# Nine score groups a batch with a shared third bank pair, and a reordered first batch, in a fused attention and feed-forward kernel

## The chip, the cores and the metric

One core of one Trainium2 chip. The metric is the device time of one execution in microseconds (us), as a median over several executions; most of them agree within 0.3%. A *call* is a session in which several kernels were timed in turn, in rounds, on one chip. Engines are named as in the profile: PE is TensorE's matmul stream and PEld its weight loads, ACT is ScalarE, DVE is VectorE, POOL is GpSimd, and SP is the queue that issues most transfers. Batches, head pairs and groups are counted from 0.

## The reference, cut to what matters

```python
# q, k, v: (8 batches, 12 heads, 448 positions, 64)
q_n = q / (norm(q) + 1e-6);  k_n = k / (norm(k) + 1e-6)
attn = softmax(q_n @ k_n.T / 0.1)
x = (attn @ v) -> (8 * 448 tokens, 768)
out = gelu(x @ w_in) @ w_out          # 768 -> 2048 -> 768
```

A batch has 12 heads, that is 6 head pairs. Each pair has 4 chunks of keys, so a batch has 24 scores. A score is two matmuls (one for each head of the pair) and one exp of 112x896.

## The kernel before: the parts that the change touches

Each of the batches 1 to 7 is an attention stage followed by the first layer of the feed-forward block (`hp`). The second layer (`op`) of earlier batches is cut into single matmuls, the *filler*, and is laid between the attention's pieces, so that TensorE has work while ScalarE computes exps. The scores go into bank pairs of TensorE's accumulator memory, two of them before the change:

```python
def scores(g, c0, n=2):                       # n scores of pair g
    qkT = qkT_t[g]
    for c in range(c0, c0 + n):
        st = ps_st.tile([128, 2, 512], F32, tag="st", ...)     # 2 buffers
        ... two matmuls into st ...
        pt = ptp.tile([CS, 2, S], BF16, tag="pt", ...)
        nc.scalar.activation(pt, st[:CS, :, :S], AF.Exp, scale=inv_tau)

def both(g, aside):                           # pairs g and g + 1
    columns(g, 0)                             # sums: 16 matmuls against ones
    reciprocals(g)                            # VectorE: transpose, reciprocal, transpose
    columns(g, 1)                             # first half of o = pt @ v
    columns(g, 2, aside=aside)                # second half
    normalise(g)                              # VectorE: x = o * reciprocal

def attention(b, fill):
    plan = {96: ((18, 8), (8, 8), (0, 10), (8, 8), (0, 10), (8, 10)),   # filler, odd batches
            128: ((22, 8), (13, 12), (0, 12), (12, 12), (0, 12), (12, 13))}[len(fill)]
    nxt = (b + 1) * HP
    for i in range(HP):                       # i: pair of the batch
        g = b * HP + i
        if i > 0:
            scores(g, 0)
        ...
        upto(scale, min(g + 4, nxt))          # GpSimd: q, k times 1/norm, up to three pairs on
        upto(transposes, min(g + 4, nxt))     # DMA transposes of them
        upto(square, nxt + min(max(i - late, 0), 3))
        run(plan[i][0])                       # filler
        if i in (2, 4):
            both(g - 2, ...)
        upto(reduce, nxt + min(max(i - 1 - late, 0), 3))
        scores(g, 2)
        if i in (0, 3):
            upto(load_v, g // 3 + 3, NV)      # values of three pairs, issued by GpSimd
        ... # loads of q and k
        run(plan[i][1])
    upto(reduce, nxt + 3); roots(2 * b + 7); both(nxt - 2, 1)

def first(b):                                 # first layer; at its end:
    ...
    scores(nxt, 0); roots(2 * b + 8)          # the next batch starts, then logarithm and root
```

`upto(f, n)` emits the next steps of `f` until n of them are out, so its place in the program fixes the place of the work in its engine's order. `square`, `reduce`, `roots` and `scale` prepare a pair; the prepared pair is then transposed by a DMA (`qkT<-qkb`). The 4 chunks of pair 3 are the batch's scores 12 to 15.

## Time and profile before

| what | before |
|---|---|
| median of 3 runs | 440.19 us (439.91 to 441.44) |
| first layer of batch 0 starts | 38.52 us |
| attention of batches 1, 3, 5, 7 (96 filler matmuls) | 30.5 to 30.6 us each |
| attention of batches 2, 4, 6 (128 filler matmuls) | 35.31 us each |
| mean granted clock of TensorE | 0.999 |

"Attention" is the time from the first score of a batch to its first matmul of the first layer.

### The profile page before, as it was taken

What the parts mean: (1) busy time and instruction counts of PE and PEld (TensorE: products, weight loads), DVE (VectorE), ACT (ScalarE), POOL (GpSimd) and SP (SyncE); (2) the same over time, 40 slices, a digit from 0 to 9 for tenths busy, and PEclk for the clock granted to TensorE, in tenths of its full rate; (3) what the DMA queues carried; (4) which work ended last, traced back from release to release, by engine and by line L of the source; (5) the groups of instructions that cost most, each with busy time, mean ns of one, the idle gap of its engine ahead of it and who ended that gap; (6) DMA issues with size and microseconds to landing.
All of it is one profiled execution on the core that took longest, in us unless ns stands there. A gap on an engine that the chain in (4) does not pass through costs nothing.

```text
span 438.1 us, 7927 instructions
## 1 busy us (share of the span) xinstructions
PE 426.8 (97%) x3294; PEld 215.7 (49%) x3294; DVE 164.8 (38%) x266; ACT 264.0 (60%) x380; POOL 203.3 (46%) x185
## 2 busy tenths in 40 slices
PE   7789999999999999999999999999999999999996
PEld 4344554445445554455544545445444554445563
DVE  4776313641355305552154501753055421341021
ACT  4796587646666467744767359655766457773300
POOL 2899834491834609291571906655190722300000
PEclk9999999999999999999999999999999999999999
DMA  9999999946683909766295843748077600911022
GB/s 201 237 241 209 180 178 211 265 105 135 109 160 88 226 4 114 171 119 149 29 159 134 159 109 53 172 121 208 1 130 153 134 2 1 132 43 31 1 72 72
DMA packets 83635, 54.97 MB, mean 125 GB/s; under 512 B 41872, under 2 KB 78608, under 8 KB 83600
## 3 DMA queue, kind: packets, MB, share of 16 engines
q1 hardware_dynamic: 66416, 42.35, 43.4%
q0 software_dynamic: 16784, 11.80, 19.1%
q8 instruction: 25, 0.41, 0.4%
q10 hardware_dynamic: 400, 0.33, 0.2%
q14 instruction: 10, 0.08, 0.1%
HBM read 45.61 MB, written 11.01 MB: 129 GB/s over the span
## 4 chain that ended last, share of the span: by engine, by line
PE 90%; DMA 5%; POOL 2%; DVE 1%; ACT 1%; SPq 0%; issue 0%; DVEq 0%
PE op L268 35%; PE hp L433 33%; PE st L206 11%; PE o L228 7%; PE sm L228 4%; DMA qk<-in_k_dram 3%; DMA v<-in_v_dram 2%; POOL qkb L176 1%; POOL sq L137 1%; SPq L107 0%; ACT pt L209 0%; DVE nq L149 0%; DVE x L246 0%; DVE rs L239 0%; DVE ot L279 0%
## 5 line engine op out<-in xcount | busy, mean ns | idle before, releaser
L209 ACT ACTIVATE pt<-st 112x896 bf16<-112x896 f32 x192 | 165.1, 913 | 50.0 <-PE st L206 49.6
L268 PE MATMUL op<-wo,g 128*128 128x384 bf16 x896 | 157.9, 327 | 0.0
L433 PE MATMUL hp<-x,wi 128*128 128x448 bf16 x768 | 147.0, 353 | 0.2 <-DVE x L246 0.2
L455 ACT ACTIVATE g<-hp 128x448 bf16<-128x448 f32 x128 | 66.9, 545 | 89.9 <-PE hp L433 89.6
L268 PEld LDWEIGHTS <-g 128*128 128x128 bf16 x896 | 81.9, 98 | 70.0 <-issue 21.0
L433 PEld LDWEIGHTS <-wi 128*128 128x128 bf16 x768 | 74.5, 98 | 72.1 <-issue 3.7
L176 POOL TENSOR_TENSOR qkb<-qk,rn 112x512 bf16<-112x512 f32 x95 | 96.8, 1045 | 11.8 <-DVE rn L167 11.7
L137 POOL TENSOR_TENSOR sq<-qk 112x1024 f32<-112x1024 f32 x44 | 82.3, 1888 | 5.8 <-DMA qk<-in_k_dram 5.6
L165 POOL TENSOR_SCALAR se<-sr 112x48 f32<-112x48 f32 x14 | 4.6, 326 | 150.2 <-ACT sr L164 150.2
L149 DVE TENSOR_REDUCE nq<-sq 112x16 f32<-112x1024 f32 x47 | 57.0, 1214 | 38.7 <-POOL sq L137 38.6
L206 PE MATMUL st<-qkT 64*112 64x448 bf16 x384 | 59.7, 374 | 2.6 <-ACT pt L209 1.9
L279 DVE COPY ot<-op 128x384 f32<-128x384 f32 x55 | 29.8, 543 | 79.2 <-PE op L268 79.2
L167 DVE RECIPROCAL rn<-se 112x48 f32<-112x48 f32 (+1 forms) x20 | 7.9, 393 | 99.7 <-POOL se L165 99.4
L228 PE MATMUL o<-pt,v 112*32 112x448 bf16 x768 | 41.8, 353 | 1.0 <-DMA v<-in_v_dram 1.0
L206 PEld LDWEIGHTS <-qkT 64*112 64x112 bf16 x384 | 21.5, 124 | 38.3 <-issue 34.5
L246 DVE TENSOR_TENSOR x<-o,rs 128x448 bf16<-128x448 f32 x48 | 27.8, 620 | 5.0 <-PE o L228 2.7
L228 PEld LDWEIGHTS <-v 112*32 112x32 bf16 x768 | 20.3, 97 | 17.1 <-DMA v<-in_v_dram 1.2
L235 DVE STREAM_TRANSPOSE tr<-sm 128x448 f32<-128x448 f32 x24 | 15.5, 646 | 34.8 <-PE sm L228 34.8
L228 PE MATMUL sm<-pt,ones 112*32 112x448 bf16 x384 | 23.1, 355 | 0.0
L323 PE MATMUL spin<-blank,ident 112*112 112x448 bf16 x46 | 13.3, 439 | 2.9 <-DVE qkT L194 1.5
L239 DVE STREAM_TRANSPOSE rs<-rc 128x448 f32<-128x448 f32 x24 | 15.5, 645 | 0.8
L120 POOL DMA_DIRECT2D v<-in_v_dram x17 | 14.0, 823 | 0.0
(37 smaller groups left out, 80.0 us busy)
## 6 DMA issues: line engine op xcount, KB each, us to landing
qk<-in_q_dram SPq DMA_DIRECT2D x48, 224.0 KB, 5.8
qk<-in_k_dram SPq DMA_DIRECT2D x47, 224.0 KB, 6.1
v<-in_v_dram POOLq DMA_DIRECT2D x15, 336.0 KB, 6.8
wi<-in_moe_w_in_dram POOLq DMA_DIRECT2D x4, 768.0 KB, 11.5
wo<-in_moe_w_out_dram POOLq DMA_DIRECT2D x4, 768.0 KB, 20.7
out_dram<-ot SPq DMA_DIRECT2D x7, 336.0 KB, 3.5
out_dram<-ot SPq DMA_DIRECT2D x8, 288.0 KB, 2.6
out_dram<-ot SPq DMA_DIRECT2D x8, 240.0 KB, 3.0
```

Source lines behind the costliest of these rows:

```text
L137: nc.gpsimd.tensor_tensor(sq, t, t, ALU.mult)
L149: nc.vector.tensor_reduce(nq, sq, mybir.AxisListType.X, ALU.add)
L176: eng.tensor_tensor(qkb[:, i].rearrange("p c h d -> p h c d"), t[:, i], rn[:, i].to_broadcast([CS, 2, NC, D]), ALU.mult)
L206: nc.tensor.matmul(st[:CS, h, :S], lhsT=qkT[rows, 1, c, :], rhs=qkT[rows, 0, :, :], start=True, stop=True)
L209: nc.scalar.activation(pt, st[:CS, :, :S], AF.Exp, scale=inv_tau)
L228: nc.tensor.matmul(bank_t[g, n][r:r + 32, :S], lhsT=w, rhs=pt_t[g + j, c][:, h, :], start=(c == 0), stop=(c == NC - 1), tile_position=(0, r))
L235: nc.vector.transpose(tr.rearrange("p b r -> p (b r)"), bank_t.pop((g, 0))[:, :S])
L246: nc.vector.tensor_tensor(x_t[b][:, p + n - 1, :], bank_t.pop((g, n))[:, :S], rs, ALU.mult)
L268: nc.tensor.matmul(ps[:, :NH], lhsT=g_t[sb][:, kf, t * 128:(t + 1) * 128], rhs=wo[:, kf, ni * NH:(ni + 1) * NH], start=(kf == 0), stop=(kf ...
L279: nc.vector.tensor_copy(ot[:, lo:hi], ps[:, :NH])
L433: nc.tensor.matmul(hps[m], lhsT=wi[:, kd, m * 128:(m + 1) * 128], rhs=x_t[b][:, kd, :], start=(kd == order[0]), stop=(kd == order[-1]))
L455: nc.scalar.activation(g_t[sb][:, m, hf * S:(hf + 1) * S], hps.pop(m), AF.Gelu)
```

## The change

The intent: fewer and larger groups of scores (3, 3, 2, 3, 2, 3, 3, 2, 3 instead of twelve of 2), so that fewer waits for exps stand in TensorE's stream. The third score of a group needs a third bank pair. It gets none of its own but shares the pair that the sums and the first half of o take, which become two halves of one tile. The filler plan is new. In the first batch, copies go ahead of roots, three spins (matmuls on zeros that only keep TensorE going) are dropped, and a value load moves into an idle time.

```diff
+    def scores(g, c0, count=2):
+        for n in range(count):
+            score(*divmod(g * NC + c0 + n, NC), n == 2)
+    def score(g, c, third):
+            pool = ps_acc if third else ps_st
+            st = pool.tile([128, 2, 512], F32, tag="third" if third else "st", ...)
 ...
     def columns(g, n, chunks=range(NC), aside=0):
+        if chunks[0] == 0 and n == 0:
+            so = ps_acc.tile([128, 2, 512], F32, tag="third", name=f"so{g}")
+            bank_t[g, 0], bank_t[g, 1] = so[:, 0], so[:, 1]
 ...
     def both(g, aside):
         columns(g, 0)
+        columns(g, 1)
         reciprocals(g)
-        columns(g, 1)
 ...
-        plan = {96: ((18, 8), (8, 8), (0, 10), (8, 8), (0, 10), (8, 10)), ...
+        plan = {96: (13, 7, 10, 7, 11, 11, 9, 10, 18),
+                128: (25, 14, 13, 14, 11, 12, 10, 10, 19)}[len(fill)]
 ...
+        for k, count in enumerate((3, 3, 2, 3, 2, 3, 3, 2, 3)):
+            if k > 0:
+                scores(b * HP, n, count)
+            if k in (4, 7):
+                both(b * HP + (0 if k == 4 else 2), ...)
+            upto(reduce, nxt + (due if late else (0, 0, 0, 0, 1, 1, 2, 3, 3)[k]))
+            for i in range(-(-n // NC), -(-(n + count) // NC)):   # pairs whose first score is in the group
+                ... scale, transposes, square, load_v, load_qk as before ...
+            n += count
+            run(plan[k])
 ...
-            scores(nxt, 0)
+            scores(nxt, 0, 3)
             roots(2 * b + 8)
 ... # first batch:
-                upto(reduce, 4)
                 roots(3)
                 upto(scale, 3)
+                upto(load_wi, 1)
 ...
-            upto(load_v, (2, 3, 3, 3, 3, 4)[g], NV)
+            upto(load_v, (3, 3, 3, 3, 3, 4)[g], NV)
 ...
+    upto(load_v, 2, NV)
+    upto(transposes, 1)
+    spin(2)
     roots(2)
     upto(scale, 2)
-    upto(load_v, 2, NV)
-    upto(load_wi, 1)
-    upto(transposes, 1)
-    spin(5)
+    upto(load_v, 3, NV)
```

More of the change, by code (lines that the diff above doesn't have):

```diff
@@ L197, in transposes @@
             nc.vector.tensor_copy(qkT, tp)
-    def scores(g, c0, n=2):
-        qkT = qkT_t[g]
-        for c in range(c0, c0 + n):
-            st = ps_st.tile([128, 2, 512], F32, tag="st", name=f"st{g}_{c}")
+    def scores(g, c0, count=2):
+        for n in range(count):
+            score(*divmod(g * NC + c0 + n, NC), n == 2)
+    def score(g, c, third):
+            qkT = qkT_t[g]
+            pool = ps_acc if third else ps_st
+            st = pool.tile([128, 2, 512], F32, tag="third" if third else "st", name=f"st{g}_{c}")
             for h in range(2):
@@ L219, in columns @@
     def columns(g, n, chunks=range(NC), aside=0):
-        if chunks[0] == 0:
-            bank_t[g, n] = (mm_tile(f"o{g + 1}", aside=aside) if n == 2 else
-                            ps_acc.tile([128, 512], F32, tag=("sm", "o")[n], name=("sm", "o")[n] + str(g)))
+        if chunks[0] == 0 and n == 0:
+            so = ps_acc.tile([128, 2, 512], F32, tag="third", name=f"so{g}")
+            bank_t[g, 0], bank_t[g, 1] = so[:, 0], so[:, 1]
+        elif chunks[0] == 0 and n == 2:
+            bank_t[g, 2] = mm_tile(f"o{g + 1}", aside=aside)
         for c in chunks:
@@ L380, in attention @@
         fill = list(fill)
-        plan = {96: ((18, 8), (8, 8), (0, 10), (8, 8), (0, 10), (8, 10)),
-                128: ((22, 8), (13, 12), (0, 12), (12, 12), (0, 12), (12, 13))}[len(fill)]
+        plan = {96: (13, 7, 10, 7, 11, 11, 9, 10, 18),
+                128: (25, 14, 13, 14, 11, 12, 10, 10, 19)}[len(fill)]
         def run(n):
@@ L389, in attention @@
         nxt = (b + 1) * HP
-        for i in range(HP):
-            g = b * HP + i
-            if i > 0:
-                scores(g, 0)
-            late = 2 if b == 1 else 0
-            if i == HP - 1 and not late:
-                roots(2 * b + 7)
-            upto(scale, min(g + 4, nxt))
-            upto(transposes, min(g + 4, nxt))
-            upto(square, nxt + min(max(i - late, 0), 3))
-            run(plan[i][0])
-            if i in (2, 4):
-                both(g - 2, 0 if len(fill) % KF else 1)
-            upto(reduce, nxt + min(max(i - 1 - late, 0), 3))
-            scores(g, 2)
-            if i in (0, 3):
-                upto(load_v, g // 3 + 3, NV)
-            if late and i == 2:
-                upto(load_qk, nxt + 4)
-            if i in (3, 4):
-                upto(load_qk, nxt + i + 2)
-            run(plan[i][1])
+        late = 2 if b == 1 else 0
+        n = red = due = 0
+        for k, count in enumerate((3, 3, 2, 3, 2, 3, 3, 2, 3)):
+            if k > 0:
+                scores(b * HP, n, count)
+            if k in (4, 7):
+                both(b * HP + (0 if k == 4 else 2), 0 if len(fill) % KF else 1)
+            upto(reduce, nxt + (due if late else (0, 0, 0, 0, 1, 1, 2, 3, 3)[k]))
+            due = red
+            for i in range(-(-n // NC), -(-(n + count) // NC)):
+                g = b * HP + i
+                if i == HP - 1 and not late:
+                    roots(2 * b + 7)
+                upto(scale, min(g + 4, nxt))
+                upto(transposes, min(g + 4, nxt))
+                upto(square, nxt + min(max(i - late, 0), 3))
+                if i in (0, 3):
+                    upto(load_v, g // 3 + 3, NV)
+                if late and i == 2:
+                    upto(load_qk, nxt + 4)
+                if i in (3, 4):
+                    upto(load_qk, nxt + i + 2)
+                red = min(max(i - late, 0), 3)
+            n += count
+            run(plan[k])
         upto(reduce, nxt + 3)
```

## The prediction

> **What bounds the kernel now.** I read the page first, then the chain that ended last, then TensorE's timeline stage by stage, then the timeline of all engines around one narrow wait. The page says who is full, from start to end and at full clock:
>
> ```profile
> PE 426.8 (97%) x3294; PEld 215.7 (49%) x3294; DVE 164.8 (38%) x266; ACT 264.0 (60%) x380; POOL 203.3 (46%) x185
> PE   7789999999999999999999999999999999999996
> PEclk9999999999999999999999999999999999999999
> PE 90%; DMA 5%; POOL 2%; DVE 1%; ACT 1%; SPq 0%; issue 0%; DVEq 0%
> ```
>
> The chain (last line) leaves TensorE only in the first batch. So a saving has to shorten TensorE's stream, and any new wait in that stream costs its full length. Batch 3 (counting from 0) shows the stream; columns are start, duration, engine, line, instruction, count:
>
> ```profile
> 159.62 0.59 PE L206 MATMUL st<-qkT 64*112 64x448 bf16 x4
> 160.13 3.10 PE L268 MATMUL op<-wo,g 128*128 128x384 bf16 x18
> 163.16 0.58 PE L206 MATMUL st<-qkT 64*112 64x448 bf16 x4
> 163.68 1.47 PE L268 MATMUL op<-wo,g 128*128 128x384 bf16 x8
> 165.09 0.83 PE L206 MATMUL st<-qkT 64*112 64x448 bf16 x4
> ```
>
> Score groups alternate with runs of second-layer matmuls as filler. From the starts: a group of two scores takes 0.52 us, a run of n filler 0.1625n + 0.10 us, one `both` (sums and two halves of o, 48 matmuls) 2.385 us. The batch ran from 159.62 to 190.18, 30.56 us, with 96 filler matmuls; the even batches carry 128 and take 35.31. Summed without waits these give 29.9 and 35.2, so the waits in a batch are worth 0.65 and 0.1 us at most. The 0.83 group is one of them: it waits for an exp.
>
> ScalarE explains it. After the last GELU it must load a table, so the first exp starts 1.96 us after the first score; then exps follow each 0.81 us, with the logarithm and root for the batch's pairs 3 to 5 behind the second exp:
>
> ```profile
> 160.28 1.28 ACT L457 ACT_TABLE_LOAD   x1
> 161.58 1.72 ACT L209 ACTIVATE pt<-st 112x896 bf16<-112x896 f32 x2
> 163.19 0.34 ACT L155 ACTIVATE lq<-nq,tiny 112x48 f32<-112x48 f32 x1
> 163.61 0.24 ACT L164 ACTIVATE sr<-lq 112x48 f32<-112x48 f32 x1
> ```
>
> Those roots feed pair 3: GpSimd scales it, a DMA transposes it, TensorE scores it. This is the narrowest place of the batch:
>
> ```profile
> 166.82 0.83 POOL L120 DMA_DIRECT2D v<-in_v_dram  x1
> 166.91 5.18 SPq L186 DMA_TRANSPOSE qkT<-qkb  x2
> ...
> 174.42 0.18 PEld L206 LDWEIGHTS <-qkT 64*112 64x112 bf16 x4 [0.32 <-DMA qkT<-qkb]
> ```
>
> The transpose is issued 7.29 us after the batch's first score, 0.09 us behind a value load, and the weight load for pair 3 stands waiting for it: the trace puts its landing at 174.18, 7.27 us after issue, 14.56 after the first score; it is needed at 14.81. In batches 2 to 7 it took 6.1, 7.3, 7.0, 5.7, 5.9 and 6.2 us. Nothing else in the kernel has so little slack.
>
> **What the Trainium skill says.** "TensorE: Matmul & The Clock Gate", section "Step-by-step: what each phase is for": weight loads may be pulled ahead, matmuls stay in program order. The trace agrees: at 165.09 the filler behind the waiting score did not start before it. So filler placed after a late score hides nothing. The page "Trainium Kernel Development and Optimization", "Key Constraints": DMAs issued from the three queues share the same 16 DMA engines and interleave. The trace agrees: value load and transpose issued together land together (the transposes issued in the first layer's stretches, with no value load beside them, took 2.9 to 5.1 us). The clock-gate page's "HAM oscillation" section warns of TensorE gaps over about 3.4 us, after which the clock is halved; no gap before exceeds 1.6 us, so the trace before cannot show it.
>
> **The change part by part.**
>
> *Nine groups instead of twelve.* A third score adds one 0.23 us step, so a group of three takes 0.75. Scores: 6x0.75 + 3x0.52 = 6.05 against 12x0.52 = 6.2; filler runs go from 10 to 9, saving 0.10. With the removed waits a batch could fall to 29.7 (96 filler) or 34.9 (128): gains of 0.8 and 0.4 us, some 4.5 us over seven batches.
>
> *But the pacing changes.* The new filler plan starts with 13 where 18 stood, then 7, 10, 7. I step through a 96-filler batch (t = 0 at its first score; an exp starts 0.44 after its score, a waiting score 0.05 after the exp that frees its bank; exps at 1.96, 2.78, 3.59, then log and root, then from 4.96 each 0.81). Group 2 could start at 2.97; its second score waits for exp 1 until 3.73, its third (third bank pair) for exp 2 until 4.55: 1.1 us lost. Group 3 loses 0.4, group 4 0.15. The fifth group is at 10.93 and 11.16; the sums behind it now share the third bank pair and wait for exp 10 until 11.81. All this makes 2.2 us of waits by the first `both`.
>
> *Pair 3 is needed earlier and prepared later.* The fifth group's second score (12 in the batch) is the first of pair 3, and it now stands before the first `both`, at 11.16 instead of 14.81. The roots now stand behind three exps: their end moves from 4.24 to 5.05, and the transpose's issue from 7.29 to 8.11. The value load still stands just before it in GpSimd's order. With the durations above it lands at 15.4, 13.8 and 14.3 in batches 3, 5, 7: TensorE waits 4.2, 2.6 and 3.1 us. In the 128 batches the score is needed at 14.14 and lands at 14.2, 15.1, 14.0: waits of 0.1, 1.0 and 0.
>
> *Late roots for the next batch.* The third square sum now stands in VectorE's order behind the second `both`, and the logarithm in ScalarE's order before the last three exps. With sums and o in one tile, the transpose of the sums starts only when the first half of o is done: 1.75 us after the first sum instead of 0.99. Then transpose, reciprocal, transpose, two products (2.87) and the reduction: it ends 5.74 after the first sum; last exp done at 8.85. TensorE gets there at 7.93: about 0.95 lost in batches 3 and 5, 0.8 in 2, 4 and 6; none in 1 and 7.
>
> *First batch.* It has TensorE's only long waits; this one is for values:
>
> ```profile
> 12.31 0.59 PE L206 MATMUL st<-qkT 64*112 64x448 bf16 x4
> 32.73 0.93 PE L228 MATMUL o<-pt,v 112*32 112x448 bf16 x14 [0.96 <-DMA v<-in_v_dram]
> ```
>
> Copies ahead of the second roots and two spins instead of five let the first score start at 10.3 instead of 12.31. But the reduction for pair 3 moves behind a copy, and its root then holds ScalarE: following the chain, of 2 us about 0.9 remain by pair 3. Value load 3 leaves GpSimd's chain and removes the 0.96 us wait at 32.73. At the end, the pair-4 sums must now wait until both products of pair 2 have read the shared tile. First layer at about 37.2 instead of 38.52: 1.3 us gained. DMA is above 90% busy in all slices to 45 us and beyond, so the transposes of batch 1 hardly move; pair 9's lands at about 70.5 (70.95 before) but is wanted at 66.7 (11.16 after a first score at 55.5). From that score to the first layer the steps above give 20.5 us: 91.0 instead of 87.3. Batch 1 turns the 1.3 gained into some 3.8 lost.
>
> *Sum.* For a 96 batch: 29.73 without waits, some 1.85 lost to pacing in groups 2 to 4 and 0.25 later, the transpose's wait (which takes the place of the exp-10 wait), the late roots. In batch 3: 29.73 + 1.85 + 0.25 + 4.2 + 0.9. Batch 3: 36.9 against 30.56 (+6.3); 5: 35.3 (+4.7); 7: 34.85 (+4.3). Batches 2, 4, 6: +0.65, +1.6, +0.5. With batch 1 at +3.8: 21.9 us. Tail unchanged. 440.2 + 21.9 = 462; I say 460, as transposes may land sooner with TensorE's stores coming later.
>
> **The rivals.** (1) The intended gain: groups are cheaper and waits vanish; 4.5 us in the batches, 1 to 3 in the first: about 434. For it: no engine but TensorE is full, and the chain is 90% TensorE. Against it: the 0.32 us wait at 174.42, which shows no slack for needing pair 3 earlier. (2) Only the exp pacing costs: the transposes land in some 3 us, as those without a value load did; then the 96 batches lose about 2 us each, late roots another 0.9 in five, the rest gains: about 448. Against it: all six transposes beside a value load took 5.7 us or more. (3) Long waits let the clock fall: each wait of over 3.4 us then costs another 1 to 2 us of half-speed matmuls; 463 to 470. (4) DMA in batch 1 is so full that wo or pairs 7 and 8 make waits too: 1 to 2 us more.
>
> **Range and chances.** The sum rests on four transposes; if each lands 2 us sooner, about 452; a clock that falls in two or three batches gives 468. So 449 to 469 around 460.0. Faster by over 2% needs below 431, more than every saving I can count: 0.02. Within 2% ends at 449, the case of the second rival: 0.11. Slower: 0.87.
>
> **What would show it.** Right: a line of st waiting for DMA qkT, once in each of batches 1, 3, 5, 7, for 2 to 4 us, the transposes issued about 8.1 us after the batch's first score; TensorE's idle total at least 12 us; first layer of batch 0 starting near 37; the six groups of three with pitches of 0.23 where they do not wait. Wrong: no idle before those scores; transposes landing under 4 us after issue; sums that start before the exp of the third bank pair; even batches below 34.9, or a first batch over 3 us shorter. A slice of PEclk below 9 in mid-kernel would speak for the third rival.

## The result, and the profile after

The changed kernel took 469.26 us (468.23 to 469.73, 4 runs) beside 440.78 us for the kernel before (4 runs, one more than in the table above). The ratio is 1.0644 (95% interval 1.0615 to 1.0674). Ratios here and below are the mean time of one kernel's fast runs over that of the other's of the same rounds, so they are not quite the ratio of the medians. Executions over 1.5% slower than the fastest of the same kernel are left out of the means. The prediction said 460, with 469 as the upper end of its range: the direction was right, the size 9 us short. The medians above differ by 28.5 us and the two profiled executions by 29.6 (spans of 438.1 and 467.7 us).

From the page after:

```profile
PEclk9899997999999998999999999999999999799999
PE 71%; ACT 10%; DMA 6%; DVE 6%; POOL 3%; issue 2%; POOLq 0%; ACTq 0%; DVEq 0%
```

TensorE's share of the chain of waits has fallen from 90% to 71%, so new waits now stand in its stream. The clock row has slices of 7 and 8 where it had only 9. To see where, I cut both traces into the attentions of the batches. Columns are the stretch, its length, the busy time of PE, PEld, DVE, ACT and POOL, then the granted clock, the DMA share and GB/s. First before, for batches 1, 3 and 4, then after, for batches 1, 3, 4, 5 and 7:

```profile
56.78:87.29 30.51, 30.51 (x290) 15.05 (x289) 12.42 (x20) 23.39 (x30) 13.63 (x12) 1.00 1.12 219
159.62:190.18 30.56, 30.52 (x290) 15.00 (x289) 14.06 (x24) 24.50 (x31) 16.78 (x16) 1.00 0.63 109
208.44:243.75 35.31, 35.31 (x321) 17.53 (x321) 14.98 (x26) 24.72 (x31) 17.81 (x17) 1.00 0.55 105
```

```profile
55.74:93.32 37.58, 33.71 (x290) 16.07 (x289) 12.32 (x20) 22.84 (x30) 13.59 (x12) 0.91 0.90 177
166.17:204.80 38.63, 32.48 (x289) 15.93 (x289) 13.26 (x22) 24.06 (x31) 17.68 (x17) 0.96 0.49 92
223.07:258.79 35.72, 35.07 (x322) 18.24 (x321) 14.44 (x24) 24.35 (x31) 17.69 (x17) 1.00 0.53 108
277.05:314.24 37.19, 32.35 (x289) 15.92 (x288) 13.27 (x22) 24.05 (x31) 17.68 (x17) 0.95 0.47 95
386.50:424.49 37.99, 33.65 (x290) 16.04 (x289) 9.68 (x18) 23.60 (x29) 7.18 (x8) 0.91 0.29 55
```

An even batch costs 0.4 to 0.5 us more than before; an odd one 6.6 to 8.1. In the odd batches alone the clock is below 1.00, at 0.91 to 0.96. Inside batch 3, TensorE's timeline shows what happens (start, duration, instruction, count, and in brackets the idle time before and what ended it):

```profile
177.06 0.40 PE L211 MATMUL st<-qkT 64*112 64x448 bf16 x2
181.64 0.55 PE L211 MATMUL st<-qkT 64*112 64x448 bf16 x2 [4.18 <-DMA qkT<-qkb]
182.12 1.68 PE L235 MATMUL so<-pt,ones 112*32 112x448 bf16 x16
183.59 1.71 PE L235 MATMUL so<-pt,v 112*32 112x448 bf16 x16
185.08 0.97 PE L235 MATMUL o<-pt,v 112*32 112x448 bf16 x16
...
187.88 0.40 PE L211 MATMUL st<-qkT 64*112 64x448 bf16 x2
```

The second score of the fifth group, the first of pair 3, waits 4.18 us for its DMA transpose. After the wait the sums take 1.68 us and the first half of o 1.71, where the second half still takes 0.97: the first two ran at half clock. From the sums to the next score is 187.88 - 182.12 = 5.76 us. The same instructions in batch 4 take 4.28, so the half clock costs 1.5 us here. In batches 1, 3, 5 and 7 the same two starts lie 6.98, 5.76, 5.56 and 6.92 us apart: 25.2 - 4 x 4.28 = 8.1 us together. The clock record has half-speed stretches at 69.11 (for 6.83 us), 181.75 (3.41), 290.98 (3.41) and 400.21 (6.83), each around the end of one of these waits, and one at 14.50 (3.41) in the first batch. The record before has none until the last microsecond.

In the waits over the whole execution (total, times, longest), one line names the transposes and another the late roots, through the exps behind them:

```profile
PE st L211 <- DMA qkT<-qkb: 13.0, 4, 4.2
PE so L235 <- ACT pt L214: 3.6, 5, 0.8
```

The transposes were issued as predicted: 8.10 to 8.11 us after the batch's first score in all seven batches. They took 5.87, 6.00, 7.32, 5.87, 6.00, 5.90 and 6.34 us (5.7 to 7.3 before). A value load was again issued 0.09 us ahead of each. The waits for them were 2.79, 4.18, 2.87 and 3.20 us in batches 1, 3, 5 and 7.

### The profile page after: what moved, and what is told of

It is laid out like the page before. It is cut to its first block, busy times and chain, and to the rows that moved or that the text cites. A ratio compares the mean times of both kernels' runs of the same rounds, so it can differ in the third digit from the quotient of the medians.

```text
span 467.7 us, 7917 instructions
## 1 busy us (share of the span) xinstructions
PE 437.0 (93%) x3291; PEld 222.2 (48%) x3291; DVE 164.8 (35%) x266; ACT 261.3 (56%) x380; POOL 204.2 (44%) x185
## 4 chain that ended last, share of the span: by engine, by line
PE 71%; ACT 10%; DMA 6%; DVE 6%; POOL 3%; issue 2%; POOLq 0%; ACTq 0%; DVEq 0%
PE hp L443 31%; PE op L275 21%; PE so L235 9%; ACT pt L214 7%; PE st L211 6%; DMA qkT<-qkb 5%; PE o L235 3%; POOL qkb L176 3%; DVE x L253 2%; DVE nq L149 1%; ACT L467 1%; DVE rs L246 1%; DMA qk<-in_q_dram 1%; DVE tr L242 1%; ACT lq L155 1%
## 5 line engine op out<-in xcount | busy, mean ns | idle before, releaser
L214 ACT ACTIVATE pt<-st 112x896 bf16<-112x896 f32 x192 | 161.9, 916 | 60.7 <-PE st L211 59.8
L176 POOL TENSOR_TENSOR qkb<-qk,rn 112x512 bf16<-112x512 f32 x95 | 97.8, 1055 | 10.1 <-DVE rn L167 10.0
L242 DVE STREAM_TRANSPOSE tr<-so 128x448 f32<-128x448 f32 x24 | 15.5, 647 | 63.2 <-PE so L235 63.0
L235 PEld LDWEIGHTS <-v 112*32 112x32 bf16 x768 | 23.2, 104 | 17.8 <-issue 6.3
L235 PE MATMUL so<-pt,ones 112*32 112x448 bf16 x384 | 26.1, 391 | 4.5 <-ACT pt L214 3.6
L235 PE MATMUL so<-pt,v 112*32 112x448 bf16 x384 | 26.0, 389 | 0.1
L235 PE MATMUL o<-pt,v 112*32 112x448 bf16 x384 | 24.7, 372 | 0.0
L155 ACT ACTIVATE lq<-nq,tiny 112x48 f32<-112x48 f32 (+1 forms) x20 | 6.6, 329 | 26.6 <-DVE nq L149 25.5
L235 PEld LDWEIGHTS <-ones 112*32 112x32 bf16 x384 | 10.1, 101 | 16.2 <-issue 12.7
L253 DVE TENSOR_TENSOR x<-o,rs 128x448 bf16<-128x448 f32 x24 | 15.0, 624 | 4.3 <-PE o L235 2.0
```

Of the source, the lines that this page charges most:

```text
L176: eng.tensor_tensor(qkb[:, i].rearrange("p c h d -> p h c d"), t[:, i], rn[:, i].to_broadcast([CS, 2, NC, D]), ALU.mult)
L235: nc.tensor.matmul(bank_t[g, n][r:r + 32, :S], lhsT=w, rhs=pt_t[g + j, c][:, h, :], start=(c == 0), stop=(c == NC - 1), tile_position=(0, r))
L242: nc.vector.transpose(tr.rearrange("p b r -> p (b r)"), bank_t.pop((g, 0))[:, :S])
L253: nc.vector.tensor_tensor(x_t[b][:, p + n - 1, :], bank_t.pop((g, n))[:, :S], rs, ALU.mult)
```

## The experiments

The theory (A): pair 3's transpose is needed earlier and issued later, runs slowly because it runs beside the value load, and the wait that this makes lets the clock fall. The rivals: (B) the exp pacing of the groups of three is the main loss; (C) the late roots for the next batch are; and the first batch may have given or taken something of its own. In each expectation the letters or words say which theory expects what. All ten kernels gave correct results.

### v_late: the value load moved behind the transposes

From the changed kernel, the first of a batch's two value loads is issued by GpSimd two pairs later (at i = 2 instead of 0), behind all of the batch's scaling and a square.

```diff
-                if i in (0, 3):
+                if i == 3:
                     upto(load_v, g // 3 + 3, NV)
+                if i == 2:
+                    upto(load_v, (g - 2) // 3 + 3, NV)
```

> The changed kernel with one edit: each batch's value load is issued behind the scaling of the batch's last pair instead of in front of the fourth transpose. Theory A (the transpose of pair 3 is needed too early and is slow because the value load runs beside it; the clock then falls because of the wait): the transpose lands 3 to 3.5 us after issue instead of 5.7 to 7.3, the wait at pair 3's first score falls from 2.8 to 4.2 us to under 0.5 us in batches 3, 5 and 7, the clock stays full there, and the time falls from 469 to 449 to 452 us. Theory B (the smaller filler runs make TensorE wait for exps; the transpose only shows a wait that would be had anyway): under 4 us, to 465 or more.

Measured: 457.94 us (454.89 to 460.05), ratio 1.041 (1.0364 to 1.0457). Pair 3's transposes took 2.89 to 2.98 us in all seven batches, where they had taken 5.9 to 7.3, and no wait for them was left. Batch 3 in the changed kernel, then in v_late:

```profile
DMA to landing us min/median/max: 7.3/7.3/7.3
```

```profile
DMA to landing us min/median/max: 2.9/2.9/2.9
```

That half of theory A is shown: with the value load beside it the transpose takes about twice as long or more. The total missed the 449 to 452 us of theory A, since my edit put the load too late and made another wait. Here are TensorE and, below it, GpSimd of batch 3:

```profile
184.82 0.37 PE L235 MATMUL so<-pt,v 112*32 112x448 bf16 x2
187.59 1.62 PE L235 MATMUL so<-pt,v 112*32 112x448 bf16 x14 [2.40 <-DMA v<-in_v_dram]
```

```profile
176.26 1.89 POOL L137 TENSOR_TENSOR sq<-qk 112x1024 f32<-112x1024 f32 x1
178.10 0.83 POOL L120 DMA_DIRECT2D v<-in_v_dram  x1
```

The load is issued at 178.10 behind a square of 1.89 us, and the second `both` waits 2.40 us for it. That wait alone was enough for a fall of the clock: half-speed stretches begin at 187.70 and 296.93. So a clock fall does not need the transposes; this wait for values had the same effect.

### warm: TensorE kept busy in the wait

Twelve spins ahead of pair 3's first score in the odd batches. They do not bring the transpose sooner; they keep the clock.

```diff
+            if k == 4 and b % 2:
+                scores(b * HP, n, 1)
+                spin(12, aside=0 if len(fill) % KF else 1)
+                scores(b * HP, n + 1, 1)
-            if k > 0:
+            elif k > 0:
                 scores(b * HP, n, count)
```

> The changed kernel with 12 blank matmuls (some 2.3 us) in batches 1, 3, 5, 7 just before pair 3's first score, so that TensorE is busy for part of the wait and the wait itself is no shorter. Theory A with the clock: the landing of the transpose moves by under 0.2 us, no half-clock stretch follows the waits, the time falls by what the half-clock stretches cost, about 8 us, to 461. Rival (the half clock is hidden beside other work, the transposes alone cost 29 us): no change, 469.

Measured: 461.86 us (461.17 to 462.58), ratio 1.0505 (1.0485 to 1.0524), so 7.4 us less than the changed kernel's 469.26 of the earlier call, by adding 48 useless matmuls. TensorE in batch 3:

```profile
176.50 2.48 PE L330 MATMUL spin<-blank,ident 112*112 112x448 bf16 x12
180.76 0.40 PE L211 MATMUL st<-qkT 64*112 64x448 bf16 x2 [1.79 <-DMA qkT<-qkb]
181.09 0.94 PE L235 MATMUL so<-pt,ones 112*32 112x448 bf16 x16
```

The score still waits for the transpose, but the sums behind it take 0.94 us instead of 1.68. No half-speed stretch follows a wait any more; the only one left before the tail is in the first batch (at 13.08, for 6.83 us). With that one longer than in the changed kernel (first layer at 38.54 instead of 37.47), the spans differ by 6.9 us and the part behind the first batch by 8.0. From the sums to the next score it is 4.28 us again in all four odd batches, so the 8.1 us worked out above for the half clock is confirmed. That the total moves by the same amount is partly chance: the sums of the odd batches also start 1.0 us sooner, all four together, and the even batches are 1.2 us longer, most of it in batch 2, which now waits 0.85 us for its transpose.

### roots_early: the roots ahead of the third score

```diff
-            scores(nxt, 0, 3)
+            scores(nxt, 0, 2)
             roots(2 * b + 8)
+            score(nxt, 2, True)
```

> The changed kernel with the roots of pairs 3 to 5 moved back to behind the second exp of a batch, the third exp behind them. Theory A: transposes are issued 7.3 instead of 8.1 us after the first score, land 0.8 us sooner, waits shrink by 0.8 us in four batches: 2.5 to 5 us less, 464 to 467, depending on how many half-clock stretches go with them. Theory B: the third score of group 2 waits 0.6 us longer, and nothing is won: 469 to 471.

Measured: 464.20 us (462.53 to 465.29), ratio 1.0545 (1.0518 to 1.0572). SP's queue issues pair 3's transpose 7.30 us after the first score again (at 172.53 in batch 3; 7.58 in batch 6), and the wait there is shorter by 0.74 us:

```profile
179.95 0.62 PE L211 MATMUL st<-qkT 64*112 64x448 bf16 x2 [3.44 <-DMA qkT<-qkb]
```

The waits in batches 1, 3, 5 and 7 are 2.32, 3.44, 2.10 and 2.37 us instead of 2.79, 4.18, 2.87 and 3.20, so the later issue was the cause of 0.5 to 0.8 us of each, and not of the rest. In return the exp of the third score runs later, and the last wait of group 2 in batch 3 grows from 0.41 to 0.96 us. The stretch of half clock stays in all four (3.41 us each), even behind the 2.10 us wait of batch 5.

### reduce_first: the third square sum ahead of the second `both`

```diff
                 scores(b * HP, n, count)
+            if k == 7 and not late:
+                upto(reduce, nxt + 3)
             if k in (4, 7):
```

> The changed kernel with the third square sum of the next batch moved ahead of the second pair of products on VectorE. If the late roots hold ScalarE before the last three exps, the waits of 0.8 to 0.95 us before the last sums go in batches 2 to 6: 3.5 to 4.5 us less, about 465. Rival (the last sums wait for TensorE's own filler or for the third bank pair): no change.

Measured: 464.58 us (460.05 to 467.29; one of its four runs was slow), ratio 1.0532 (1.0476 to 1.0589). The waits of the last sums for exps, 3.6 us over five batches, are gone, so theory C is right as far as it goes: the late roots cost some 4 us and no more. The total, 4.7 us less, is no measure of it by itself: in the profile batch 7 gains 3.2 us, as no half-speed stretch follows its wait, and batch 4 has a new wait of 1.52 us for its transpose. The spread of this kernel follows its clock: its fast runs had mean clocks of 0.988, 0.978 and 0.978 and took 460.05, 464.15 and 465.01 us.

Batch 7 of its profile is telling. Its score waited 2.82 us, longer than some waits behind which the clock fell, and the clock did not fall. I cut the trace there along the 3.41 us grid of the section on the clock below (columns as before):

```profile
394.62:398.03 3.41, 2.03 (x13) 0.78 (x11) 0.56 (x1) 3.29 (x4) 3.41 (x4) 1.00 1.20 157
398.03:401.45 3.42, 1.98 (x38) 1.10 (x42) 0.00 (x0) 0.92 (x1) 0.25 (x1) 1.00 1.13 210
```

The wait lies across the border of two windows and leaves TensorE busy for 2.03 and 1.98 us of each.

### What decides whether the clock falls

All half-speed stretches of the changed kernel start on one grid: 69.11 - 14.50 = 16 x 3.413 us, 181.75 - 69.11 = 33 x 3.413, and 290.98 - 181.75 as well as 400.21 - 290.98 = 32 x 3.413. Here is each of the 3.41 us windows just before a fall in the changed kernel:

```profile
11.09:14.50 3.41, 1.29 (x12) 0.67 (x11) 2.48 (x5) 2.75 (x5) 3.41 (x3) 1.00 1.17 251
65.70:69.11 3.41, 1.26 (x8) 0.48 (x6) 0.56 (x1) 2.52 (x4) 2.96 (x3) 1.00 1.35 182
178.34:181.75 3.41, 0.11 (x2) 0.11 (x2) 0.00 (x0) 0.38 (x1) 3.41 (x4) 1.00 1.26 111
287.57:290.98 3.41, 0.77 (x5) 0.18 (x3) 0.22 (x1) 2.02 (x3) 3.41 (x4) 1.00 1.35 180
396.80:400.21 3.41, 0.99 (x7) 0.32 (x4) 0.45 (x1) 2.25 (x3) 2.61 (x3) 1.00 1.44 168
```

TensorE is busy for 0.11 to 1.29 us of 3.41. The Trainium skill, "TensorE: Matmul & The Clock Gate", section "What's actually happening", says that a free-running window of 3413 ns is watched; the grid agrees. What the traces add is that a window need not be idle. In all twelve profiles, cut along their grids at full clock and without the last 10 us, every window after the first batch that was followed by a fall was busy for at most 1.30 us (roots_early, 285.57 to 288.98), and every other one for at least 1.98. So it matters how a wait lies on the grid: the 2.10 us wait of roots_early lies in that one window, the 2.82 us wait above in two. In the first batch no such line can be drawn. Both of these windows, in first_only and in warm_plan (two kernels below), were followed by a fall:

```profile
9.17:12.58 3.41, 2.05 (x16) 0.99 (x16) 3.37 (x7) 2.60 (x7) 2.73 (x3) 1.00 1.17 284
20.32:23.73 3.41, 2.29 (x23) 1.11 (x25) 1.86 (x5) 2.88 (x6) 3.41 (x4) 1.00 1.12 233
```

The kernel before was busy for 2.15 us from 7.55 to 10.96, and its clock did not fall. What decides there stays open. Where the grid lies, and with it some of the cost, may change from run to run; with one profile of each kernel this is not shown.

### first_only: the first batch's edits alone

From the kernel before, with only the first-batch part of the diff.

> The kernel before with the edits of the first batch alone (copies ahead of the second roots, two spins for five, value load 3 and weight load 1 moved), twelve score groups kept. If the first batch's part is worth what it was meant for: first layer 1 to 1.5 us sooner than 38.52, 438.5 to 439.3 against 440. A half-clock stretch of 3.4 or 6.8 us near 13 us, as in all runs with these edits so far, that eats the rest. Rival (the DMA queue is full, so batch 1 waits for its transposes and gives all of it back): no change.

Measured over five rounds: 438.70 us (438.44 to 439.79), ratio 0.997 (0.9945 to 0.9996). In the profile the first layer starts at 38.04 us (before: 38.52) and the attentions of batches 1 to 7 are within 0.02 us of what they were before. The profile has a half-speed stretch of 6.83 us from 12.58, where the profile of the kernel before has none. The dropped spins are one possible reason, which the next run tries. But 7 of the 11 runs of the kernel before in this call had a mean clock of 0.990 to 0.992 as well, where the profile of first_only has 0.990, so the kernel before is not free of such stretches and the reason is not shown. The three runs with a mean clock of 0.996 took 438.44 to 438.64 us, the three with 0.990 to 0.992 took 438.76 to 439.79.

### first_warm: the same with spins given back

```diff
                 upto(load_wi, 1)
+                spin(4)
                 scores(g, 2, 1)
+                spin(8)
```

> The same with 12 more spins in TensorE's two idle stretches between 11 and 14 us. If the clock fell because of these: no half-clock stretch before the end, first layer at 36.0 to 37.0, 437.5 to 438.5. Rival: the first batch hangs on GpSimd and ScalarE, not on TensorE's clock: within 0.3 us of first_only.

Measured over five rounds: 439.51 us (438.80 to 439.99), ratio 0.9982 (0.9956 to 1.0008). In the profile the first layer starts at 37.39 us with no half-speed stretch ahead of it, 1.1 us sooner than before but short of the 36.0 to 37.0 expected, and the timed runs are no better than those of first_only. The gain of the first batch is thus between nothing and 0.5% and not settled further.

### mended: the changed kernel with its three faults removed

The value load behind the scaling of the last pair but ahead of the square that delayed it in v_late, the third square sum first, and the spins of first_warm.

```diff
+            if k == 7 and not late:
+                upto(reduce, nxt + 3)
 ...
                 upto(transposes, min(g + 4, nxt))
+                if i == 2:
+                    upto(load_v, (g - 2) // 3 + 3, NV)
                 upto(square, nxt + min(max(i - late, 0), 3))
-                if i in (0, 3):
+                if i == 3:
                     upto(load_v, g // 3 + 3, NV)
```

> The changed kernel with nine groups in all batches, but the value load behind the scaling of the last pair and ahead of the square sums' inputs, the reduction ahead of the second products, and the extra spins in the first batch. Pacing by exps alone should then be left: odd batches 32.1 us (30.56 before), even ones 34.9 (35.31), no half-clock stretch, no wait for a transpose over 0.5 us: 442 to 444. If nine groups are good once the waits are mended: under 440.

Measured: 445.13 us (444.51 to 445.86), ratio 1.0117 (1.008 to 1.0153). The attentions of batches 1 to 7 took 32.65, 34.94, 32.11, 34.94, 32.11, 34.94 and 32.11 us at a mean clock of 1.000, and pair 3's transposes 2.90 to 2.97. The last transposes of each batch, now issued 0.09 us or less behind the load, took 5.5 to 7.5 us, and nothing waited for them: the slowness moved with the load. TensorE in batch 3, with the same group as in the profile after:

```profile
171.25 0.59 PE L211 MATMUL st<-qkT 64*112 64x448 bf16 x4
172.15 0.94 PE L235 MATMUL so<-pt,ones 112*32 112x448 bf16 x16 [0.31 <-ACT pt L214]
...
176.42 0.78 PE L211 MATMUL st<-qkT 64*112 64x448 bf16 x6
```

The two scores run on without a wait, and from the sums to the next score it is 4.27 us. So two reordered steps and a dozen spins take back 24 of the 29 us (469.26 - 445.13, medians of two calls). Batch 1 is 0.54 us longer than the other odd ones because its second half of o waits 0.59 us for a bank that VectorE still copies from. What remains against the kernel before is theory B at its true size: 32.11 - 30.56 = 1.55 us in an odd batch, while an even batch is 0.37 us shorter than before. The odd batches have too little filler between their first groups for exps that follow each other at 0.81 us; the timeline has waits of 0.2 to 0.4 us for exps in groups 2, 3 and at the sums. This is the price of nine groups with this filler plan (13, 7, 10, 7 at first, 18 at the end). A plan with more of the 96 in front was not tried with nine groups, so how much of the 1.55 us belongs to the groups themselves is open.

### mix: nine groups in even batches, twelve in odd ones

Mended, but the odd batches call the loop of the kernel before (with the sums and o still sharing a tile).

```diff
-            attention(b, fill)
+            (attention_twelve if b % 2 else attention)(b, fill)
...
-            scores(nxt, 0, 3)
+            scores(nxt, 0, 2 if b % 2 == 0 else 3)
```

> As mended, but twelve groups with the old filler plan in the batches with 96 filler matmuls, nine groups in those with 128. If a third bank pair pays only where there is filler enough between the groups: odd batches 30.5, even ones 34.8 to 34.9, first layer near 36.5: 436 to 437.5, faster than both kernels. Rival: even batches at 35.3 or more, then no better than first_warm.

Measured over five rounds: 438.99 us (438.33 to 440.08), ratio 0.9975 (0.9949 to 1.0001). The even batches took 34.94 us as expected, but the odd ones 30.75 to 30.82, some 0.25 more than in the kernel before. In the same call first_only took 438.70 and first_warm 439.51, so the nine groups of the even batches bring no gain that the spread of the runs would show.

### mix_plan and warm_plan: a new filler plan for the odd batches, with a shared tile and with own tiles

Both give the odd batches' twelve groups the plan below. mix_plan is mix with it; warm_plan is first_warm with it (twelve groups in all batches, the sums and o in tiles of their own).

```diff
-        plan = {96: ((18, 8), (8, 8), (0, 10), (8, 8), (0, 10), (8, 10)),
+        plan = {96: ((18, 10), (9, 9), (0, 9), (9, 9), (0, 9), (8, 6)),
```

> The mixed kernel (nine groups in even batches, twelve in odd ones) with the filler of the odd batches spread by the exps: 18, 10, then 9 in each gap, 6 at the end. If the odd batches' short waits (0.25 once, 0.1 four times, and 0.25 for a filler bank) come from gaps of 8, which are 0.05 to 0.1 us shorter than two exps, they go from 30.81 to 30.0 to 30.3 us, the even ones stay at 34.94: 2 to 3 us under the mixed kernel, about 436.5. Rival (the waits only move to the group behind): 438.5 to 439.

> The kernel before with the first batch's edits and extra spins and the same spread of filler in the odd batches, twelve groups everywhere, sums and o in tiles of their own: odd batches 29.9 to 30.1 us, even ones 35.31 unchanged, about 437. It shows what the plan gives without the third bank pair: if it is as fast as the mixed kernel with the plan, the third bank pair pays for nothing.

Measured over five rounds: mix_plan 440.97 us (440.39 to 441.56), ratio 1.0031 (1.001 to 1.0052), odd batches 31.09 to 31.28; warm_plan 438.32 us (436.90 to 439.31), ratio 0.9964 (0.9942 to 0.9986), odd batches 30.25 to 30.44. So with this plan the third bank pair pays for nothing: without it the kernel is some 2.6 us faster. The same plan gained 0.1 to 0.3 us an odd batch in one kernel and lost 0.3 to 0.5 in the other. TensorE behind the first `both` of batch 3, in mix_plan and then at the same place in warm_plan:

```profile
172.26 0.50 PE L275 MATMUL op<-wo,g 128*128 128x384 bf16 x2
173.50 1.30 PE L275 MATMUL op<-wo,g 128*128 128x384 bf16 x7 [0.74 <-DVE x L253]
```

```profile
172.99 1.78 PE L268 MATMUL op<-wo,g 128*128 128x384 bf16 x9
```

In mix_plan a filler run that needs a new bank waits 0.74 us until VectorE's products have read o out of it. The prediction had worked out that the reciprocals start 1.75 - 0.99 = 0.76 us later with the shared tile, and so the products do; the wait is of that size. Whether the shared tile or the order in which `both` emits its steps holds the reciprocals back was not separated. warm_plan has the lowest median of all kernels here and is clear of the kernel before by its interval, but at 0.4% it is the same within the 2% mark. Its profile has a half-speed stretch at 23.73 that its two fastest runs (436.90 and 437.59 us, at clocks of 1.000 and 0.999) seem not to have had.

## Why the prediction was right or wrong

By its own terms, over the whole kernel (us). The measured column is from the profiles: waits from the changed kernel's trace, pacing from mended against before.

| term | predicted | measured |
|---|---|---|
| first layer of batch 0 starts sooner | -1.3 | -1.05 |
| groups and exp pacing, four odd batches | +5.1 | +6.2 |
| cheaper groups, three even batches | -1.2 | -1.1 |
| waits for pair 3's transposes | 13.7 odd, 1.1 even | 13.0 odd, up to 0.25 each even |
| late roots | +4.2 | +3.6 |
| clock | 0 in the sum (rival 3) | +8.1 |
| sum | 21.6 (21.9 in the text) | about 29, of 29.6 |

The 21.9 of the text is off its own parts: its even batches, at 0.65, 1.6 and 0.5, are some 0.5 us above what it counts for them (0.4 saved, then the wait, then 0.8), and its batch 7 is 0.1 below. The odd pacing is predicted as 4 x (29.73 + 1.85 + 0.25 - 30.56) and measured as 3 x 1.55 and 1.59 in batch 1, whose 37.58 us leave 32.09 without its wait of 2.79 and its half clock of 2.7.

**The failed step** is the clock. The text put it among the rivals ("Long waits let the clock fall ... 463 to 470") and left it out of the sum, although the sum itself contained waits of 3.8 and 4.2 us, both over the 3.4 us that the rival asked for, and two more of 2.6 and 3.1. By its own rule two falls of 1 to 2 us each belonged in the sum, which makes 464 to 466 of its 462. Measured were four, at 2.7, 1.5, 1.3 and 2.6 us, because less than 3.4 us of idle time suffices. With this term the sum would have been 30 us. That 30 lies so near the measured 29.6 is partly luck: the pacing was 1.1 us too low, the waits for transposes 1 to 2 us and the late roots 0.6 us too high.

**What was right.** The place of the loss, pair 3's transpose, was named with its issue time (8.11 predicted, 8.10 to 8.11 measured) and its cause, the value load (v_late: 2.9 us without it). The waits were 4.2, 2.6 and 3.1 us predicted for batches 3, 5 and 7, and 4.18, 2.87 and 3.20 measured. Batch 1 was predicted at 3.8 and measured at 2.79, because its transpose landed sooner than assumed (5.87 us after issue). The waits of group 2 were put at 1.1 us and came to 1.2 (two scores at a distance of 0.81 us each instead of 0.23 and 0.19).

**What was a little off.** The third score adds 0.19 us, not 0.23, so a group of three takes 0.71 us. The late roots cost 0.65 or 0.81 us a batch rather than 0.8 to 0.95. Even batches hardly waited for a transpose, where 1.1 us had been counted for them.

**What the sum missed for the intent.** Rival 1 hoped for a kernel that gains. mended shows that even with these three faults removed the nine groups, with this filler plan, gain 0.37 us in an even batch and lose 1.55 in an odd one. The odd batches of mix and mix_plan are slower than the same twelve groups with tiles of their own; whether the shared pair or the order of the steps makes this was not separated.

What stays open: how much the first batch's edits gain, since the mean clock there differs from run to run; what share of a window must be busy in the first batch to keep the clock; what nine groups would cost in odd batches with another filler plan; and some 0.5 us of the 29.6, which no single wait shows.

## What to carry to other kernels

Before regrouping an engine's stream, list for every piece that moves forward when its inputs land, and what runs beside their transfer: here the cost came from a transpose that had 0.25 us of slack before (14.81 - 14.56), and a value load issued 0.09 us ahead of it. When a sum contains waits of some microseconds on TensorE, the half-speed work behind each of them belongs in the sum, at 1.3 to 2.7 us here, and not among the rivals. A few spins in a wait that can't be removed are worth their place (7.4 us here), and the place of one load in GpSimd's order is worth more than that (11.3 us in v_late, although it made a new wait there).

## What the Trainium skill lacked or had wrong

- "TensorE: Matmul & The Clock Gate", section "HAM oscillation — how this bites in real kernels": its rule, no gaps of TensorE over about 3.4 us, is too lenient here. The clock halved behind waits of 2.10, 2.40 and 2.79 us, after 3.41 us windows that were busy for 1.30, 1.01 and 1.26 us, and stayed behind one of 2.82 us that lay across two windows (2.03 and 1.98 us busy).
- The same page, section "What's actually happening", gives the free-running window of 3413 ns, and the starts of the half-speed stretches agree with it (multiples of 3.413 us). It gives no share of a window below which it counts as idle. Here, after the first batch, windows busy for at most 1.30 us were followed by a fall and those busy for at least 1.98 were not, but in the first batch one of 2.29 us was. The stretches here lasted 3.41 or 6.83 us, one or two windows.
- "Trainium Kernel Development and Optimization", section "Key Constraints", says that the queues share the DMA engines, but no page puts a number on what that does to a DMA transpose: here 2.9 us with no value load beside it and 5.9 to 7.3 us with one issued 0.09 us ahead.
